# Attention ahead of two feed-forward layers: converting weights two steps later, and sums, loads, maxima and keys in a new order

## The chip, the cores and the metric

The kernel runs on one NeuronCore of a Trainium2 chip. The metric is the device time of one execution in microseconds (us), taken from the runs as they are; a further execution was recorded by the hardware profiler. Engines are named as the profile names them: PE (TensorE, matrix products), PEld (its weight loads), DVE (VectorE), ACT (ScalarE), POOL (GpSimd), SP (the queue that issues all DMAs). Each engine works through its own instructions strictly in the order in which the program lists them, and waits for others through semaphores.

## What is computed

The reference, cut to what matters (batch 2, 8 heads, 768 positions, head size 64; all float32):

```python
k_sum = k.reshape(B, H, nb, 32, D).max(axis=3)          # nb = 24 blocks
v_sum = v.reshape(B, H, nb, 32, D).mean(axis=3)
scores_l = scale * q @ k.T, kept where |i - j| < 16
scores_s = scale * q @ k_sum.T + log(32)
a = softmax(concat(scores_l, scores_s))
x = a @ concat(v, v_sum)                                 # 1536 tokens x 512
x = (g(x @ w_in)) @ w_out,  g(h) = h * cos(h)            # 512 -> 2048 -> 512
out = layernorm(h * softmax(h)) * g_ln @ w_out2, h = x @ w_in2   # 512 -> 1024 -> 512
```

The weights arrive as 64-bit floats, seen as pairs of 32-bit words, and are turned into float32 on the chip.

## The kernel before

**Stages.** Attention runs first, then the two feed-forward layers (FFN). The change lies in attention alone, and in the few FFN products that attention takes in between its own.

**Tiles of attention.** Two heads of one batch are a pair; there are 8 pairs (n = 0 to 7). A pair's 768 positions are three groups of four tiles of 64 queries, so there are 24 groups G = 3n + g. Each query tile sees a window of 96 keys and the 24 block summaries, 120 columns.

**The loop over steps.** Lines 663 to 741 are one loop with 29 steps (0 to 28), a software pipeline written out by hand: in step s the group s + 1 gets its scores while older groups are at later stages. In the order of the program a step holds:

- PE: the scores of group s + 1 (`emit_s`, L561, 16 products); the transposes of the probabilities of group s - 4 (`emit_t`, L598); where s = 3n + 2, the transposes of keys and queries of pair n + 2 (`emit_k` L494, `emit_q` L533); `fill` (L355: some first products of the FFN, L277, as the table `FILL` says); the product with v of group s - 5 (`emit_av`, L613); the block sums of v of a pair, in the steps that `VSUM_AT` lists (`sum_v`, L472, 24 products).
- DVE: the maxima of group s (`emit_max`, L572), the block maxima of keys (`emit_ksum`, L506) where the step has them, the sums of group s - 2 (`emit_sum`, L585, L586), the **join** of a weight's two words (`join_one`, L169), and, in every step with s = 3n + 1, the copies that lay the heads of keys and of queries of pair n + 2 side by side (`pair_k`, `pair_q`, both L426, tiles `kg` and `qg`). PE transposes these copies in the following step.
- ACT: the ends of the key windows (`emit_kx_ends`, L522, L525; first in the step for the pairs in `KX_FIRST`), the exponential of group s - 1 (L581), the high part of a joined weight (L186), the eviction of the transposed probabilities (`emit_at`, L603), the two **rebias** operations on a weight's words (`rebias_one`, L162, L163), the eviction of the result into `X` (L627), then key windows (`emit_kx`, L515), query rows (L547), high parts of `X` (L246) and the scaled block sums (`scale_v`, L480) where the step has them.
- POOL: the low part of a split weight (L187), the subtraction of the maxima of group s (L576), the normalisation of group s - 2 (L591), and the low part of a slice of `X` in steps 7, 10, 13 and 16 (`XS`, L247).
- SP: the loads of weights, keys, queries and v, and the copies that **place** the block sums into the tile of v (`place_vsum`, L487, at the start of the step after `scale_v`).

**A weight's way.** Attention converts the first 8 weight tiles. In a step listed in `WSTEPS` a tile is opened (`weights.bits`: its load, and that of the next one, is issued if it was not before). In the step after it ACT rebiases and DVE joins it; in the step after that ACT and POOL split it into a high and a low part. `load(0)` is issued apart, in step 2.

**PSUM banks.** Scores, transposed probabilities and results use four banks. The tile `qk` (three banks, one buffer) holds a pair's transposed keys and queries until ACT and DVE have read them. The bank `h` holds the block sums of v of pairs 0 to 5 and, from step 15 on, the first FFN product; the block sums of pairs 6 and 7 use `qk`. From step `QK_DONE` on, the three banks of `qk` are given to FFN products.

Two lines fix the order on DVE that the steps follow: `weights.finish()` (the join, L711) stands ahead of `pair_k(n + 2)` and `pair_q(n + 2)` (L732, L733) in the loop's body.

Of the kernel before, what the change touches and what calls it, by code (L numbers as in the profile page):

```python
# [7 lines left out]
F32 = mybir.dt.float32  # L8
# [16 lines left out]
def strided(t, offset, dims):  # L25

    return bass.AP(t.tensor, t.offset + offset, [list(t.ap[0])] + [list(d) for d in dims])
# [7 lines left out]
def fused_kernel(  # L35
# [15 lines left out]
    P = 128  # L51
    B, H, S, D = q.shape
# [39 lines left out]

    wide = w_in.dtype == mybir.dt.int64
    LOWEST = -3.0e38
    WSTEPS = (4, 7, 10, 13, 15, 16, 18, 19)
    XS = (7, 10, 13, 16)
    IDLE = (0, 0, 0)
    DVE_X = 19
    DVE_NORM = 99
    LAST = 5  # L100
    QK_DONE = 20
    REBIAS = float(2.0 ** -112)
    NEGATIVE = float(2.0 ** 32)
    TOP3 = float(0.936 * 2.0 ** -29)
# [165 lines left out]
    def h_products(step):  # L270
        fg, tb, f = work[step]
        h = h_of[step] = h_tile(step)
        m = 0
        for c in range(KC):
            for (a, b_) in PASSES:
                w = weights.done[w1[fg][0][c]]
                nc.tensor.matmul(  # L277
                    h, lhsT=w[:, a, f * P:(f + 1) * P], rhs=xs_of[tb, c][:, b_, :],
                    start=(m == 0), stop=(m == 3 * KC - 1))
                m += 1  # L280
                yield
# [54 lines left out]
    ps_h0 = ps_stack.enter_context(tc.tile_pool(name="ps_h0", bufs=1, space=PSUM))  # L336
    qk_stack = ps_stack.enter_context(ExitStack())
    ps_qk = qk_stack.enter_context(tc.tile_pool(name="ps_qk", bufs=1, space=PSUM))
# [3 lines left out]
    def warm_up(n):  # L342

        if not n:
            return
        idle = idles[0]
        t = ps_h0.tile([P, 512], F32, tag="h", name="idle")
        for _ in range(n):
            nc.tensor.matmul(t, lhsT=idle[:, 0:P], rhs=idle, start=True, stop=True)


    FILL = {15: 3, 16: 3, 17: 3, 18: 3, 20: 4, 21: 4, 22: 4, 23: 4, 24: 4, 25: 4, 26: 4, 27: 4, 28: 4}
    early = (x for step in range(GF) for x in h_products(step))

    def fill(step):  # L355

        if step == QK_DONE:
            qk_stack.close()
            ps_h[0] = ps_stack.enter_context(tc.tile_pool(name="ps_h", bufs=3, space=PSUM))
        for _ in range(FILL.get(step, 0)):  # L360
            next(early, None)
# [23 lines left out]
    def attention():  # L385
        st = ExitStack()
        with st:
# [41 lines left out]
            def pair_k(n):  # L429
                k_t[n] = side_by_side(k_t[n], "kg", nc.gpsimd if n == 1 else nc.vector)  # L430
# [30 lines left out]
            def blocks_of(t):  # L461
                at = FIRST if t == 0 else FINAL if t == NT - 1 else MID + 2 * HALF - 2 * (t % HALF)
                return strip[0:WIN, at:at + D]

            def sum_v(n):

                o = (ps_h0 if n < 6 else ps_qk).tile(
                    [P, 512] if n < 6 else [P, 2, 2, S // 2], F32, tag="h" if n < 6 else "qk", name="vsum")
                o = (o if n < 6 else o[:, 0, 0])[:, 0:P]
                for t in range(HALF):  # L470
                    for c in range(2):
                        nc.tensor.matmul(  # L472
                            o[D * c:D * c + D], lhsT=blocks_of(HALF * c + t),
                            rhs=v_t[n][0:WIN, HALF * c + t].rearrange("p j d -> p (j d)"),
                            start=(t == 0), stop=(t == HALF - 1))
                vs_t[n] = o
# [27 lines left out]
            def emit_ksum(n):  # L504
                ksum = io.tile([P, NS], F32, tag="ksum", name="ksum")
                nc.vector.tensor_reduce(  # L506
                    out=ksum, in_=strided(qk_t["k", n], 0, [[BLOCK // 2, NS], [S // 2, 2], [1, BLOCK // 2]]),
                    op=ALU.max, axis=AX.XY)
                ks_t[n] = ksum
# [56 lines left out]
            def emit_max(G):  # L566
                g = G % GPP
                sm = sm_t[G] = sms[G % NSM]
                sps = ss_t.pop(G)
                mx = sm_p.tile([P, NG], F32, tag="mx", name="mx")  # L570
                for i in range(NG):
                    nc.vector.tensor_tensor_reduce(  # L572
                        out=sm[:, i, 0:KW], in0=sps[:, i, :], in1=mask[:, (NG * g + i > 0) + (NG * g + i == NT - 1), :], scale=1.0, scalar=LOWEST,
                        op0=ALU.add, op1=ALU.max, accum_out=mx[:, i:i + 1])
                sm = sm[:, :, 0:KW]
                nc.gpsimd.tensor_tensor(  # L576
                    out=sm, in0=sm, in1=mx.unsqueeze(2).to_broadcast([P, NG, KW]), op=ALU.subtract)
# [5 lines left out]
            def emit_sum(G):  # L583
                ss = sm_p.tile([P, NG], F32, tag="ss", name="ss")
                nc.vector.tensor_reduce(out=ss, in_=sm_t[G], op=ALU.add, axis=AX.X)  # L585
                nc.vector.reciprocal(out=ss, in_=ss)  # L586
                sum_t[G] = ss
# [41 lines left out]
            NPAIR = B * NP  # L629
            NGR = NPAIR * GPP  # L630
# [26 lines left out]


            LX, LN, LT, LA = 1, 2, 4, 5
            KX_FIRST = (1, 2, 3, 4, 5)  # L660
            VSUM_AT = {1: 0, 5: 1, 8: 2, 10: 3, 13: 4, 14: 5, 16: 6, 19: 7}
            VLOAD_AT = {1: 1, 4: 2, 6: 3, 8: 4, 10: 5, 13: 6, 16: 7}
            for step in range(NGR + LA):
                n, g = divmod(step, GPP)
                summed = LN <= step < NGR + LN
                ahead = 1 if step == 1 else n + 1 if g == 0 and 0 < n < NPAIR - 1 else 0

                warm_up(IDLE[g] if step < min(FILL) else 0)
                if step - 1 in VSUM_AT:
                    place_vsum(VSUM_AT[step - 1])  # L670
                if step + 1 < NGR:
                    emit_s(step + 1)
                if step == 0:
                    pair_k(1)
                    emit_max(0)
                    pair_q(1)
                    emit_k(1)
                    emit_q(1)
                if LT <= step < NGR + LT:
                    emit_t(step - LT)  # L680
                if g == 2 and n + 2 < NPAIR:
                    emit_k(n + 2)
                    emit_q(n + 2)
                fill(step)
                if step >= LA:
                    emit_av(step - LA)
                if step in VSUM_AT:
                    sum_v(VSUM_AT[step])

                if g == 1 and n in KX_FIRST:  # L690
                    emit_kx_ends(n + 1)
                if step == NGR:
                    emit_at(step - LT)
                if LX <= step < NGR + LX:
                    emit_exp(step - LX)
                weights.split()
                if 0 < step < NGR:
                    emit_max(step)
                if LT <= step < NGR + LT and step != NGR:
                    emit_at(step - LT)  # L700
                if g == 1 and 0 < n < NPAIR - 1 and n not in KX_FIRST:
                    emit_kx_ends(n + 1)
                if ahead:
                    emit_ksum(ahead)
                if summed:
                    emit_sum(step - LN)
                if step == NGR + 3:
                    emit_x(step - LA)
                weights.rebias()
                drain(step - NGR, 0)  # L710
                weights.finish()  # L711
                if summed:
                    emit_norm(step - LN)
                if step >= LA and step != NGR + 3:
                    emit_x(step - LA)
                drain(step - NGR, 1)
                if ahead:
                    emit_kx(ahead)
                if step == 1:
                    emit_kx_ends(1)  # L720
                    emit_qx(1)
                if g == 2 and n + 2 < NPAIR:
                    emit_qx(n + 2)
                if step == 2:
                    weights.load(0)
                if step in WSTEPS:
                    weights.bits()
                for c in range(KC):
                    if step == XS[c]:
                        xs_of[0, c] = split_x(0, c, xs_a)  # L730
                if g == 1 and n + 2 < NPAIR:
                    pair_k(n + 2)  # L732
                    pair_q(n + 2)  # L733

                if g == 1 and n + 3 < NPAIR:
                    load_k(n + 3)
                    load_q(n + 3)
                if step in VLOAD_AT:
                    load_v(VLOAD_AT[step])
                if step in VSUM_AT:  # L740
                    scale_v(VSUM_AT[step])

# [682 lines left out]
```

## Time and profile before

| what | us |
|---|---|
| median of 3 runs (477.47, 478.20, 482.47) | 478.2 |
| the profiled execution | 477.52 |
| its span, first to last instruction | 475.7 |
| attention in it: PE's last attention product ends, FFN's line 319 begins | 97.11 |
| busy in the span: PE / DVE / ACT / POOL | 467.1 / 317.6 / 314.4 / 227.3 |

Busy time is the time in which an engine has an instruction under way. In a timeline a row gives the start in us from the span's start, the duration in us, engine, line, operation and tiles (written <- read); a number in brackets is the idle time of the engine just before it, with what ended it. Neighbouring instructions overlap a little at their ends, so the distance of two starts is the better measure of what one costs.

### The profile page before, as it was taken

What the parts mean: (1) busy time and instruction counts of PE and PEld (TensorE: products, weight loads), DVE (VectorE), ACT (ScalarE), POOL (GpSimd) and SP (SyncE); (2) the same over time, 40 slices, a digit from 0 to 9 for tenths busy, and PEclk for the clock granted to TensorE, in tenths of its full rate; (3) what the DMA queues carried; (4) which work ended last, traced back from release to release, by engine and by line L of the source; (5) the groups of instructions that cost most, each with busy time, mean ns of one, the idle gap of its engine ahead of it and who ended that gap; (6) DMA issues with size and microseconds to landing.
All of it is one profiled execution on the core that took longest, in us unless ns stands there. A gap on an engine that the chain in (4) does not pass through costs nothing.

```text
span 475.7 us, 8064 instructions
## 1 busy us (share of the span) xinstructions
PE 467.1 (98%) x2899; PEld 384.2 (81%) x2899; DVE 317.6 (67%) x754; ACT 314.4 (66%) x558; POOL 227.3 (48%) x230
## 2 busy tenths in 40 slices
PE   8999999999999999999999999999999999999997
PEld 4788877788888888888888888888888888888886
DVE  3989965663554456566464647474799999988930
ACT  3689888757675866556665456664872448888891
POOL 2689988424322222222223723655105878795450
PEclk9999999999999999999999999999999999999999
DMA  7999875001223222233222122110210031436351
GB/s 210 269 230 248 219 182 177 12 1 45 90 95 116 99 88 90 90 113 108 90 88 88 45 88 87 49 45 1 88 45 1 22 84 28 119 59 113 88 133 68
DMA packets 61304, 46.52 MB, mean 98 GB/s; under 512 B 42704, under 2 KB 53712, under 8 KB 61264
## 3 DMA queue, kind: packets, MB, share of 16 engines
q1 hardware_dynamic: 61264, 46.01, 34.3%
q8 instruction: 23, 0.38, 0.3%
q14 instruction: 17, 0.14, 0.1%
HBM read 36.43 MB, written 3.15 MB: 83 GB/s over the span
## 4 chain that ended last, share of the span: by engine, by line
PE 88%; POOL 4%; DVE 3%; DMA 2%; ACT 1%; issue 1%; SPq 0%; DVEq 0%; POOLq 0%
PE y L319 27%; PE h L277 27%; PE h L1074 14%; PE h L907 12%; PE sps L561 2%; PE ops L613 2%; PE aps L598 1%; POOL sm L576 1%; PE vsum L472 1%; POOL sm L591 1%; DMA qt<-in_q_dram 1%; DMA raw<-in_moe_w_out_dram 1%; POOL w L187 1%; DVE sm L572 1%; DVE ksum L506 1%
## 5 line engine op out<-in xcount | busy, mean ns | idle before, releaser
L277 PE MATMUL h<-xs,w 128*128 128x512 f32 x576 | 141.2, 391 | 0.0
L319 PE MATMUL y<-gs,w 128*128 128x512 f32 x576 | 138.2, 389 | 0.0
L319 PEld LDWEIGHTS y<-gs,w 128*128 128x128 f32 x576 | 108.0, 188 | 22.4
L277 PEld LDWEIGHTS h<-xs,w 128*128 128x128 f32 x576 | 107.2, 188 | 21.6
L187 POOL TENSOR_TENSOR w<-s,w 128x512 fp32r<-128x512 f32 x32 | 41.7, 1303 | 97.1 <-ACT w L186 95.1
L286 ACT ACTIVATE r<-h 128x512 int32<-128x512 f32 x48 | 28.6, 597 | 87.1 <-PE h L277 87.1
L291 DVE SCALAR_TENSOR_TENSOR r<-r,h 128x512 f32<-128x512 int32 x48 | 32.9, 686 | 71.0 <-ACT r L286 70.8
L1074 PE MATMUL h<-w,ls 128*128 128x512 f32 (+1 forms) x312 | 66.8, 374 | 0.0
L169 DVE SCALAR_TENSOR_TENSOR s<-raw 128x512 int32<-128x512 int32 x48 | 37.7, 786 | 40.5 <-ACT raw L163 39.2
L1074 PEld LDWEIGHTS h<-w,ls 128*128 128x128 f32 x312 | 55.3, 188 | 10.9 <-POOL ls L1051 0.6
L907 PE MATMUL h<-w,xo 128*128 128x512 f32 x252 | 58.7, 390 | 0.0
L907 PEld LDWEIGHTS h<-w,xo 128*128 128x128 f32 x252 | 47.1, 188 | 9.7
L296 ACT ACTIVATE r<-r,half_pi 128x512 f32<-128x512 f32 x48 | 34.5, 720 | 5.4 <-DVE r L291 5.3
L307 DVE TENSOR_TENSOR gs<-h,gs 128x512 fp32r<-128x512 f32 x48 | 32.6, 680 | 5.3 <-ACT gs L306 5.3
L301 DVE TENSOR_TENSOR h<-h,r 128x512 f32<-128x512 f32 x48 | 33.0, 688 | 4.0 <-ACT r L296 3.9
L162 ACT ACTIVATE raw<-raw 128x512 f32<-128x512 f32 x48 | 32.0, 667 | 1.0 <-DMA raw<-in_moe_w_out_dram 1.0
L778 POOL TENSOR_TENSOR w<-s,w 128x512 fp32r<-128x512 f32 x14 | 17.9, 1294 | 30.9 <-ACT w L777 30.9
L163 ACT ACTIVATE raw<-raw 128x512 int32<-128x512 uint32 x48 | 32.0, 666 | 0.0
L576 POOL TENSOR_TENSOR sm<-sm,mx 128x480 f32<-128x480 f32 x24 | 24.7, 1031 | 8.7 <-DVE mx L572 8.7
L306 ACT ACTIVATE gs<-h 128x512 fp32r<-128x512 f32 x48 | 28.2, 587 | 0.4 <-DVE h L301 0.3
L1044 ACT ACTIVATE s<-turned 128x1024 uint16<-128x1024 uint16 x20 | 26.5, 1367 | 2.3 <-POOL xo L895 1.8
L591 POOL TENSOR_TENSOR sm<-sm,ss 128x480 f32<-128x480 f32 x24 | 27.2, 1134 | 1.4 <-DVE ss L586 1.3
(105 smaller groups left out, 667.8 us busy)
## 6 DMA issues: line engine op xcount, KB each, us to landing
raw<-in_moe_w_in_dram SPq DMA_DIRECT2D x24, 512.0 KB, 3.7
raw<-in_moe_w_out_dram SPq DMA_DIRECT2D x24, 512.0 KB, 3.4
vt<-in_v_dram SPq DMA_DIRECT2D x16, 240.0 KB, 5.3
kt<-in_k_dram SPq DMA_DIRECT2D x8, 384.0 KB, 3.2
qt<-in_q_dram SPq DMA_DIRECT2D x8, 384.0 KB, 7.8
out_dram<-osb SPq DMA_DIRECT2D x11, 256.0 KB, 2.1
vt<-vm SPq DMA_DIRECT2D x16, 72.0 KB
vt<-in_v_dram SPq DMA_DIRECT2D x16, 48.0 KB, 6.0
```

The source lines that it names most:

```text
L162: nc.scalar.activation(out=hw, in_=hw, func=AF.Prelu, scale=REBIAS, alpha=NEGATIVE)
L163: nc.scalar.activation(out=lw, in_=lw.bitcast(U32), func=AF.Copy, scale=TOP3)
L169: nc.vector.scalar_tensor_tensor(out=self.f32[i], in0=t[:, :, 1], scalar=3, in1=t[:, :, 0], op0=ALU.logical_shift_left, op1=ALU.bitwise_or)
L187: nc.gpsimd.tensor_tensor(out=w[:, 1, :], in0=f, in1=as32(w[:, 0, :]), op=ALU.subtract)
L277: nc.tensor.matmul(h, lhsT=w[:, a, f * P:(f + 1) * P], rhs=xs_of[tb, c][:, b_, :], start=(m == 0), stop=(m == 3 * KC - 1))
L291: nc.vector.scalar_tensor_tensor(out=r, in0=r.bitcast(I32), scalar=TWO_PI, in1=h_of[step], op0=ALU.mult, op1=ALU.subtract)
L296: nc.scalar.activation(out=r, in_=r, func=AF.Sin, scale=-1.0, bias=half_pi)
L301: nc.vector.tensor_tensor(out=h, in0=h, in1=r, op=ALU.mult)
L307: nc.vector.tensor_tensor(out=gs[:, 1, :], in0=r, in1=as32(gs[:, 0, :]), op=ALU.subtract)
L319: nc.tensor.matmul(y[e], lhsT=w[:, a, e * P:(e + 1) * P], rhs=gs[:, b_, :], start=(f == 0 and i == 0), stop=(f == GF - 1 and i == 2))
L907: nc.tensor.matmul(banks_of[p][BANK[m]], lhsT=x[:, a, s0:s0 + P], rhs=w2_of[m, c][:, b_, :], start=c == j == 0, stop=c == 1 and j == 2)
L1074: nc.tensor.matmul(o, lhsT=ls_of[t][f // 4][:, a, s0:s0 + P], rhs=w[:, b_, cols], start=(f == 0 and i == 0), stop=(f == NF2 - 1 and i == 2))
```

## The change

The diff is whole. What it does:

- `WSTEPS`: each of the eight weights is opened, rebiased, joined and split two steps later. Rebias and join, which stood in steps 5, 8, 11, 14, 16, 17, 19 and 20, stand in 7, 10, 13, 16, 18, 19, 21 and 22. `load(0)` moves from step 2 to step 4.
- `FILL`: the 48 FFN products that stood in steps 15 to 18 (3 each) and 20 to 28 (4 each) stand in steps 19 to 28 (6, 6, 5, 5, 5, 5, 4, 4, 4, 4). `QK_DONE` moves from 20 to 21.
- `sum_v`: pair 6's block sums use bank `h`, as pairs 0 to 5 do. `VSUM_AT`: pair 1's sums move from step 5 to 4, pair 4's from 13 to 12, pair 5's from 14 to 15, pair 6's from 16 to 18, pair 7's from 19 to 20.
- `VLOAD_AT`: the loads of v of pairs 2, 4 and 5 move one step later, and stand behind the placing of pairs 1, 2 and 3 on SP.
- Step 2: `emit_max(3)` (of step 3) comes right after `emit_max(2)`; the block maxima and the windows of the third pair's keys (`emit_ksum(2)`, `emit_kx(2)`), of step 3 before, come in step 2, ahead of that pair's query rows on ACT.
- `KX_FIRST` takes in 6: the key ends of pair 7 come first in step 19 on ACT.

```diff
--- before.py
+++ after.py
@@ -92,13 +92,13 @@
 
     wide = w_in.dtype == mybir.dt.int64
     LOWEST = -3.0e38
-    WSTEPS = (4, 7, 10, 13, 15, 16, 18, 19)
+    WSTEPS = (6, 9, 12, 15, 17, 18, 20, 21)
     XS = (7, 10, 13, 16)
     IDLE = (0, 0, 0)
     DVE_X = 19
     DVE_NORM = 99
     LAST = 5
-    QK_DONE = 20
+    QK_DONE = 21
     REBIAS = float(2.0 ** -112)
     NEGATIVE = float(2.0 ** 32)
     TOP3 = float(0.936 * 2.0 ** -29)
@@ -349,7 +349,7 @@
             nc.tensor.matmul(t, lhsT=idle[:, 0:P], rhs=idle, start=True, stop=True)
 
 
-    FILL = {15: 3, 16: 3, 17: 3, 18: 3, 20: 4, 21: 4, 22: 4, 23: 4, 24: 4, 25: 4, 26: 4, 27: 4, 28: 4}
+    FILL = {19: 6, 20: 6, 21: 5, 22: 5, 23: 5, 24: 5, 25: 4, 26: 4, 27: 4, 28: 4}
     early = (x for step in range(GF) for x in h_products(step))
 
     def fill(step):
@@ -464,9 +464,9 @@
 
             def sum_v(n):
 
-                o = (ps_h0 if n < 6 else ps_qk).tile(
-                    [P, 512] if n < 6 else [P, 2, 2, S // 2], F32, tag="h" if n < 6 else "qk", name="vsum")
-                o = (o if n < 6 else o[:, 0, 0])[:, 0:P]
+                o = (ps_h0 if n < 7 else ps_qk).tile(
+                    [P, 512] if n < 7 else [P, 2, 2, S // 2], F32, tag="h" if n < 7 else "qk", name="vsum")
+                o = (o if n < 7 else o[:, 0, 0])[:, 0:P]
                 for t in range(HALF):
                     for c in range(2):
                         nc.tensor.matmul(
@@ -657,13 +657,13 @@
 
 
             LX, LN, LT, LA = 1, 2, 4, 5
-            KX_FIRST = (1, 2, 3, 4, 5)
-            VSUM_AT = {1: 0, 5: 1, 8: 2, 10: 3, 13: 4, 14: 5, 16: 6, 19: 7}
-            VLOAD_AT = {1: 1, 4: 2, 6: 3, 8: 4, 10: 5, 13: 6, 16: 7}
+            KX_FIRST = (1, 2, 3, 4, 5, 6)
+            VSUM_AT = {1: 0, 4: 1, 8: 2, 10: 3, 12: 4, 15: 5, 18: 6, 20: 7}
+            VLOAD_AT = {1: 1, 5: 2, 6: 3, 9: 4, 11: 5, 13: 6, 16: 7}
             for step in range(NGR + LA):
                 n, g = divmod(step, GPP)
                 summed = LN <= step < NGR + LN
-                ahead = 1 if step == 1 else n + 1 if g == 0 and 0 < n < NPAIR - 1 else 0
+                ahead = step if step in (1, 2) else n + 1 if g == 0 and 1 < n < NPAIR - 1 else 0
 
                 warm_up(IDLE[g] if step < min(FILL) else 0)
                 if step - 1 in VSUM_AT:
@@ -694,16 +694,20 @@
                 if LX <= step < NGR + LX:
                     emit_exp(step - LX)
                 weights.split()
-                if 0 < step < NGR:
+                if 0 < step < NGR and step != 3:
                     emit_max(step)
+                if step == 2:
+                    emit_max(3)
                 if LT <= step < NGR + LT and step != NGR:
                     emit_at(step - LT)
                 if g == 1 and 0 < n < NPAIR - 1 and n not in KX_FIRST:
                     emit_kx_ends(n + 1)
-                if ahead:
+                if ahead and step != 2:
                     emit_ksum(ahead)
                 if summed:
                     emit_sum(step - LN)
+                if step == 2:
+                    emit_ksum(2)
                 if step == NGR + 3:
                     emit_x(step - LA)
                 weights.rebias()
@@ -721,7 +725,7 @@
                     emit_qx(1)
                 if g == 2 and n + 2 < NPAIR:
                     emit_qx(n + 2)
-                if step == 2:
+                if step == 4:
                     weights.load(0)
                 if step in WSTEPS:
                     weights.bits()
```

## Rows read from the trace of the kernel before

**Rows 1.** The page, part 1: busy us of each engine

```profile
PE 467.1 (98%) x2899; PEld 384.2 (81%) x2899; DVE 317.6 (67%) x754; ACT 314.4 (66%) x558; POOL 227.3 (48%) x230
```

**Rows 2.** Windows: span, busy PE, PEld, DVE, ACT, POOL, granted clock, DMA

```profile
5.88:97.11 91.23, 86.98 (x1203) 70.52 (x1201) 71.56 (x287) 72.35 (x145) 67.96 (x63) 1.00 0.72 191
...
130.00:200.00 70.00, 70.00 (x311) 57.96 (x310) 36.90 (x57) 46.33 (x86) 16.24 (x13) 1.00 0.30 98
```

**Rows 3.** Waits of PE, 5 to 100 us: total, times, longest

```profile
...
PE sps L561 <- ACT kx L525: 1.2, 1, 1.2
...
PE vsum L472 <- ACT kx L522: 0.8, 1, 0.8
PE aps L598 <- POOL sm L591: 0.3, 1, 0.3
...
```

**Rows 4.** Timeline of PE, steps 5 to 8: start, us, [idle <-releaser]

```profile
21.29 1.04 PE L561 MATMUL sps<-kx,qx 64*64 64x120 f32 x16 [1.17 <-ACT kx L525]
...
24.16 0.87 PE L533 MATMUL qk<-ident,qg 128*128 128x128 f32 x6 [0.39 <-DVE qg L426]
...
25.48 1.48 PE L472 MATMUL vsum<-vt,strip 96*64 96x128 f32 x24
26.89 1.04 PE L561 MATMUL sps<-kx,qx 64*64 64x120 f32 x16
...
29.06 1.04 PE L561 MATMUL sps<-kx,qx 64*64 64x120 f32 x16
...
31.22 1.04 PE L561 MATMUL sps<-kx,qx 64*64 64x120 f32 x16
...
33.34 0.82 PE L533 MATMUL qk<-ident,qg 128*128 128x128 f32 x6
```

**Rows 5.** Timeline of DVE, step 16: join, copies of keys and queries

```profile
62.69 0.69 DVE L169 SCALAR_TENSOR_TENSOR s<-raw 128x512 int32<-128x512 int32 x1 [3.71 <-ACT raw L163]
63.30 0.55 DVE L426 COPY kg<-kt 128x768 f32<-128x768 f32 x1
63.77 1.63 DVE L426 COPY qg<-qt 128x768 f32<-128x768 f32 x1
```

**Rows 6.** Timeline of ACT in step 16: rebias

```profile
61.39 0.71 ACT L162 ACTIVATE raw<-raw 128x512 f32<-128x512 f32 x1
61.96 0.70 ACT L163 ACTIVATE raw<-raw 128x512 int32<-128x512 uint32 x1
```

**Rows 7.** Timeline of PE, step 17: the last pair's queries

```profile
65.46 0.88 PE L533 MATMUL qk<-ident,qg 128*128 128x128 f32 x6 [0.44 <-DVE qg L426]
```

**Rows 8.** Timeline of ACT in step 7

```profile
31.41 0.61 ACT L603 ACTIVATE at<-aps 120x512 f32<-120x512 f32 x1
31.89 0.41 ACT L627 ACTIVATE X<-ops 128x256 f32<-128x256 f32 x1
```

**Rows 9.** DVE lines 169 and 426, 14 to 97 us: ns min/median/max

```profile
L169 DVE SCALAR_TENSOR_TENSOR s<-raw x8: 691/714/1384, 25.6 to 78.6; 128x512 int32<-128x512 int32 x8
...
L426 DVE COPY qg<-qt x6: 560/1339/1634, 15.1 to 63.8; 128x768 f32<-128x768 f32 x6
```

**Rows 10.** Timelines of DVE and POOL: copy of queries in step 1, POOL's next

```profile
15.06 0.56 DVE L426 COPY qg<-qt 128x768 f32<-128x768 f32 x1 [0.42 <-DMA qt<-in_q_dram]
...
16.51 0.99 POOL L576 TENSOR_TENSOR sm<-sm,mx 128x480 f32<-128x480 f32 x1 [2.95 <-DVE mx L572]
```

**Rows 11.** DMA packets in 0 to 20.5 us and in 0 to 21 us

```profile
DMA packets 9577, 4.69 MB, mean 229 GB/s; under 512 B 5051, under 2 KB 9575, under 8 KB 9575
...
DMA packets 9654, 4.74 MB, mean 226 GB/s; under 512 B 5052, under 2 KB 9649, under 8 KB 9652
```

**Rows 12.** Timeline of SP: placing pair 1's block sums

```profile
28.35 1.66 SPq L487 DMA_DIRECT2D vt<-vm  x2
```

**Rows 13.** The page, part 6: DMA issues, KB each, us to landing

```profile
vt<-in_v_dram SPq DMA_DIRECT2D x16, 240.0 KB, 5.3
```

**Rows 14.** The page, part 5: the subtraction of a split weight on POOL

```profile
L187 POOL TENSOR_TENSOR w<-s,w 128x512 fp32r<-128x512 f32 x32 | 41.7, 1303 | 97.1 <-ACT w L186 95.1
```

## The prediction

> **What bounds the kernel now.** I read the page's busy times first. PE is busy for 467.1 of 475.7 us [rows 1], so time can only come or go where PE has a gap, and the windows say where to look: from 130 us on a stretch of 70 us holds 70.00 us of PE, while attention, from 5.88 to 97.11 us, holds 86.98 of 91.23 [rows 2]. Everything behind attention is one unbroken row of products, so whatever moves the end of attention moves the end of the kernel by as much. Next the waits of PE inside attention [rows 3]: one of 1.2 us for the key windows, one of 0.8 for key ends, one of 0.3 for a normalised group. The timeline puts them in place: 1.17 us ahead of the scores of step 5, and 0.39 for copied queries in the same step; without extras a step takes 29.06 to 31.22 = 2.16 us of PE, and the block sums of v add 25.48 to 26.89 = 1.41 [rows 4]. So attention is PE's work plus small gaps, and the question is which gaps go and which come.
>
> The row that decides my forecast is step 16, the only step of before in which a join and the copies of the next keys and queries meet. DVE stood still for 3.71 us until ACT had rebiased, then joined (62.69), copied keys (63.30) and queries (63.77, 1.63 us) [rows 5]. ACT's two rebias operations had begun at 61.39 and ended at 61.96 + 0.70 = 62.66 [rows 6], 0.03 us ahead of the join. PE, one step on, waited 0.44 us for those queries [rows 7], although its own step 16 was long (three FFN products and the sums of a pair).
>
> **The change, part by part.**
>
> *Conversions two steps later.* This removes nothing: eight rebias pairs, joins and splits stay. But the joins that stood in steps 5, 8, 11 and 14 come to stand in 7, 10 and 13 (and the one of step 16 is again in 16), and 7, 10, 13 and 16 are the very steps with `pair_k` and `pair_q`, behind the join in DVE's order. Queued behind the waiting join are those two copies and the next maxima; for the copies waits PE, with all its later work behind. Step 7, from the step's start T on PE: ACT's order there is the same as before up to the eviction L603, after which its next instruction began at 31.89, that is T + 2.83 [rows 8, 4]. There the rebias now goes in: 61.96 - 61.39 + 0.70 = 1.27 us, ending at T + 4.10. Join from T + 4.13, 0.61 to the keys (T + 4.74), 0.47 to the queries (T + 5.21), then a copy of queries of 1.34, the median [rows 9]: T + 6.55, and PE takes it 0.05 later, at T + 6.60. PE would be ready for these transposes at 33.34 in before, T + 4.28 [rows 4]. Wait A: 2.3 us. Step 10 has the sums of pair 3 besides, so PE is ready at T + 4.28 + 1.41 = 5.69: wait B 0.9. Steps 13 and 16 are plain steps of 2.16 now (the sums of pairs 4, 5 and 6 have left 13, 14 and 16 for the steps ahead or later), and with sums at the end of the step before, ACT has its key windows behind it; what holds ACT is then PE's own transposes, some 1.6 into the step, one eviction (31.89 - 31.41 = 0.48, [rows 8]) and the rebias, so the join begins at about T + 3.4, the queries are ready at T + 5.87, PE is ready at T + 4.28: waits C and D 1.6 each. Sum 2.3 + 0.9 + 1.6 + 1.6 = 6.4 us.
>
> Bounds. Below: ACT never behind in any of the four steps (join at T + 3.4) and the copy at its shortest, 0.56: queries at T + 5.1, waits 0.8 + 0 + 0.8 + 0.8 = 2.4. Above: join at its longest, 1.38, and copy at 1.63 [rows 9]: 1.06 more in each step, 6.4 + 4.2 = 10.6. I take 6.4, since the join of step 16 ran at its short length and the median of the copies is a long one.
>
> The copy of queries took 0.56 in step 1, where POOL was idle for 2.95 us up to 16.51, and 1.34 or more in the others [rows 10]. The Trainium skill, Advanced Engine Details and Errata, section VectorE Performance Modes, notes that VectorE's second SBUF port is shared with GpSimd, so that the two block each other in VectorE's two-port modes. By that rule the copy is long just where POOL has work beside it, as `XS` gives it in these four steps; were POOL idle during them, the waits would come to 6.4 - 4 x 0.78 = 3.3.
>
> *Third keys and fourth maxima, sums of pair 1 in step 4.* I take it that the key windows come no sooner: ACT now holds them, and with them its wait for the keys' maxima, ahead of the query rows and the exponential, which it did in that wait before. But the sums of pair 1, 1.41, now stand on PE inside the gap of 1.17. They need v of pair 1. Its packets are of 256 bytes; the count of packets under 512 bytes stands at 5051 at 20.5 us and rises by 1 to 21 [rows 11], so it has arrived by about 20.7. PE is free at 21.29 - 1.17 = 20.12, would run the sums from 20.7 to 22.1, and start the scores of step 5 there. From those scores to step 6 it was 26.89 - 21.29 = 5.60 [rows 4], less the sums and the wait of 0.39 that falls away: 3.80, so step 6 starts at 25.9. Gain 1.0. With v there by 20.12 the queries' copy still ends near 24.1, and 24.16 + (26.89 - 24.16 - 1.41) = 25.5 is the best, gain 1.4; with v at 21.5 it is 0.2. The order of maxima costs nothing: both scores are there, and POOL's next normalisation still ends just ahead of its transposes.
>
> *Seventh sums in bank `h`, later sums, key ends first.* The sums of pairs 6 and 7 no longer wait behind key ends in `qk`: the 0.8 goes. The 0.44 of step 17 goes too, being counted anew in wait D. What is late next is the first FFN product of step 19, which needs ACT's eviction of pair 6's sums from `h`, at the end of a full ACT step; PE reaches it 1.5 into step 19: I take nothing, 1.0 at most.
>
> *First FFN products later.* 48 before and after, no cost by themselves. Five instead of four in steps 23 and 24 put PE's work ahead of the transposes that waited 0.3 for POOL [rows 3]: gain 0.3.
>
> *Loads of v behind placing.* On SP, v of pair 2 now stands behind the placing of pair 1, which waits for sums that end at 22.1 and takes 1.66 [rows 12]; it goes out from about 24.1, with the keys and queries of later pairs behind it. A load of v lands 5.3 us after its issue [rows 13], by 30; the sums that need it stand in step 8, behind the queries of 33.34 [rows 4]. The weight loads queued with it are needed two steps later than before. Cost nothing; were that cover gone, PE would wait for v as long as it lands behind 33.3.
>
> Sum on the profiled execution: 477.5 + 6.4 - 1.0 - 0.8 - 0.4 - 0.3 = 481.4 us. The profiled execution lies 0.7 below the median of the runs shown, inside their spread, so I forecast 481.4.
>
> **The rivals.**
>
> *Gaps go and none comes (not slower).* If the joins find their words ready or the copies stay ahead of PE, as with the joins of steps 8, 11 and 14 that never reached PE, all gains stand: 477.5 - 2.5 = 475.0. Against it: those joins had no copies behind them, and step 16 has. It decides from the point where the join starts before T + 1.8 in a plain step.
>
> *Long joins and copies.* All four waits at their upper bounds, 10.6, give 477.5 + 10.6 - 2.5 = 485.6. For it: POOL, freed of waits, works beside DVE more. Against: the blocked DVE starves POOL too.
>
> *Short copies.* POOL lives on what DVE hands it; if DVE's wait for the join leaves POOL idle as in step 1, the copies take 0.56 as there: 481.4 - 4 x 0.78 = 478.3. Against: POOL's split of `X` follows the same rebias on ACT and falls on the copy. The skill's rule on the shared port is what would make it so.
>
> *The tail.* Two more weights are split on POOL in steps 22 and 23, 1.3 us each [rows 14], ahead of the last subtractions; PE already waits 0.3 there. If the last of them lands on that path: 481.4 + 1.3 + 0.3 = 483.0.
>
> **How the numbers follow.** Forecast 0.58; no new gap 0.12; long copies 0.13; short copies 0.07; tail 0.10. The forecast's own range, with each wait half a microsecond off, is 479.4 to 483.4. The range 475.5 to 485.0 leaves out most of the first rival and more than half of the second, together some 0.2. A change of 1%, 4.8 us, is what a measurement of this kernel can tell from none: faster than that needs 473.4, below the best case, 0.03; slower, above 483.0, is the second rival, half of the tail and the upper edge of the forecast, 0.23; within 0.74.
>
> **What would show it.** Right: in the waits of PE, keys (L494) and queries (L533) for DVE L426 four times, together 5 to 7 us, in the steps 8, 11, 14 and 17; in DVE's timeline a join ahead of the copies each time, idle before it for ACT L163; no wait of PE for L522 and none of over 1 us for L525; attention's end near 101.0 instead of 97.11. Wrong: PE's keys and queries without waits, or a wait of PE for v (DMA), for ACT L480 in step 19, or for POOL L591 in the tail of over 0.5 us; a granted clock below full anywhere.

## The result, and the profile after

| what | before | after |
|---|---|---|
| median of 9 runs each (lowest, highest), us | 478.20 (477.19, 482.47) | 483.69 (482.14, 485.34) |
| profiled execution, us | 477.52 | 483.99 |
| attention's end, where line 319 begins, us | 97.11 | 103.12 |

The ratio of after to before is 1.010, with a 95% interval from 1.0067 to 1.0133. The change makes the kernel some 5 us slower, and the interval lies on both sides of the 1% mark. Of the 6.5 us between the profiled executions 6.0 had come about by the end of attention.

After: the page's busy time [rows 1], then the waits of PE inside attention, 5 to 110 us [rows 3] (us in total, times, longest):

```profile
PE 470.0 (97%) x2899; PEld 385.8 (80%) x2899; DVE 318.1 (66%) x754; ACT 314.2 (65%) x558; POOL 225.0 (47%) x230
```

```profile
PE qk L494 <- DVE kg L426: 3.5, 4, 1.5
PE qk L533 <- DVE qg L426: 2.7, 4, 0.7
PE vsum L472 <- DMA vt<-in_v_dram: 0.3, 1, 0.3
PE aps L598 <- POOL sm L591: 0.3, 1, 0.3
...
```

The waits for key windows (L525, 1.2) and key ends (L522, 0.8) are gone, the 0.3 for POOL stands, and the copies are waited for eight times, 6.2 us together. PE's busy time rose by 2.9 us although it has the same 2899 products: some of them ran longer, as the windows below show, or lost the overlap with the product ahead of them.

After: timeline of PE [rows 4]. Each L561 row is the start of a step (the first scores, then steps 6 to 8, 9, 11, 12 and 13 to 15), and L494 and L533 are the transposes of copied keys and queries:

```profile
9.31 1.86 PE L561 MATMUL sps<-kx,qx 64*64 64x120 f32 x32 [0.23 <-DVE qx L543]
...
25.21 1.04 PE L561 MATMUL sps<-kx,qx 64*64 64x120 f32 x16
27.38 1.04 PE L561 MATMUL sps<-kx,qx 64*64 64x120 f32 x16
29.54 1.04 PE L561 MATMUL sps<-kx,qx 64*64 64x120 f32 x16
...
32.68 0.87 PE L494 MATMUL qk<-ident,kg 128*128 128x128 f32 x6 [1.52 <-DVE kg L426]
34.23 1.54 PE L533 MATMUL qk<-ident,qg 128*128 128x128 f32 x6 [0.68 <-DVE qg L426]
...
38.42 1.04 PE L561 MATMUL sps<-kx,qx 64*64 64x120 f32 x16
...
44.06 1.04 PE L561 MATMUL sps<-kx,qx 64*64 64x120 f32 x16
...
48.87 1.04 PE L561 MATMUL sps<-kx,qx 64*64 64x120 f32 x16
...
52.35 1.04 PE L561 MATMUL sps<-kx,qx 64*64 64x120 f32 x16
54.52 1.04 PE L561 MATMUL sps<-kx,qx 64*64 64x120 f32 x16
57.02 0.87 PE L494 MATMUL qk<-ident,kg 128*128 128x128 f32 x6 [0.89 <-DVE kg L426]
58.58 0.88 PE L533 MATMUL qk<-ident,qg 128*128 128x128 f32 x6 [0.68 <-DVE qg L426]
60.00 1.04 PE L561 MATMUL sps<-kx,qx 64*64 64x120 f32 x16
```

Before, the same view gave the length of such steps without a wait: step 8, with block sums, 36.01 - 31.22 = 4.79 (its start is in [rows 4]), and step 11, without, 45.13 - 41.66 = 3.47:

```profile
36.01 1.04 PE L561 MATMUL sps<-kx,qx 64*64 64x120 f32 x16
...
41.66 1.04 PE L561 MATMUL sps<-kx,qx 64*64 64x120 f32 x16
...
45.13 1.04 PE L561 MATMUL sps<-kx,qx 64*64 64x120 f32 x16
```

So step 8 of after, 38.42 - 29.54 = 8.88, lost 4.1 us; step 11, 4.81, lost 1.3; step 14, 5.48, lost 2.0; and step 17 (5.49 from 65.64 to 71.13) 2.0 again. That is 9.4 us of lost time where the view of waits shows 6.2 of idle time. The difference has two parts. Step 8 has a slow stretch. These are the windows of after; the columns are stretch, length, busy PE, PEld, DVE, ACT, POOL, then the granted clock, DMA share and GB/s:

```profile
34.00:36.00 2.00, 1.77 (x12) 1.44 (x14) 1.97 (x14) 0.00 (x0) 2.00 (x2) 0.50 0.86 203
36.00:38.00 2.00, 2.00 (x36) 2.00 (x33) 0.62 (x7) 1.09 (x2) 2.00 (x3) 0.65 0.47 169
```

Behind the gaps of 1.52 and 0.68 us the granted clock fell to 0.50, the 1.2 GHz level, and the transposes of queries took 1.54 in place of 0.82. The other part is 0.2 us for each wait, which the experiment with the split of `X` shows below.

After: DVE in steps 7 and 16 [rows 5], and POOL beside the first:

```profile
31.47 0.69 DVE L169 SCALAR_TENSOR_TENSOR s<-raw 128x512 int32<-128x512 int32 x1 [1.66 <-ACT raw L163]
32.07 0.55 DVE L426 COPY kg<-kt 128x768 f32<-128x768 f32 x1
32.54 1.63 DVE L426 COPY qg<-qt 128x768 f32<-128x768 f32 x1
...
66.94 0.69 DVE L169 SCALAR_TENSOR_TENSOR s<-raw 128x512 int32<-128x512 int32 x1 [2.35 <-ACT raw L163]
67.55 0.55 DVE L426 COPY kg<-kt 128x768 f32<-128x768 f32 x1
68.02 1.64 DVE L426 COPY qg<-qt 128x768 f32<-128x768 f32 x1
```

```profile
32.30 1.46 POOL L247 TENSOR_TENSOR xs<-X,xs 128x512 fp32r<-128x512 f32 x1 [1.09 <-ACT xs L246]
```

Join, copy of keys and copy of queries stand in this order behind ACT's rebias, and DVE is idle until it comes. Steps 10 and 13 show the same three rows (44.68 and 55.80, idle 3.33 and 2.35).

### The profile page after: what moved, and what is told of

Read it like the earlier page. It is cut to its first block, busy times and chain, and to the rows that moved or that the text cites. A ratio compares the mean times of both kernels' runs of the same rounds, so it can differ in the third digit from the quotient of the medians.

```text
span 482.2 us, 8067 instructions
## 1 busy us (share of the span) xinstructions
PE 470.0 (97%) x2899; PEld 385.8 (80%) x2899; DVE 318.1 (66%) x754; ACT 314.2 (65%) x558; POOL 225.0 (47%) x230
## 4 chain that ended last, share of the span: by engine, by line
PE 84%; DVE 5%; ACT 4%; DMA 3%; issue 2%; POOL 1%; SPq 1%; POOLq 0%; ACTq 0%; DVEq 0%
PE y L319 27%; PE h L277 26%; PE h L911 12%; PE h L1078 10%; PE sps L561 2%; PE ops L613 2%; PE vsum L472 1%; PE aps L598 1%; DVE qg L426 1%; DMA vt<-in_v_dram 1%; PE qk L533 1%; DMA qt<-in_q_dram 1%; ACT at L603 1%; ACT kx L515 1%; DMA vt<-vm 1%
## 5 line engine op out<-in xcount | busy, mean ns | idle before, releaser
L247 POOL TENSOR_TENSOR xs<-X,xs 128x512 fp32r<-128x512 f32 x10 | 14.0, 1405 | 28.8 <-ACT xs L246 28.8
L591 POOL TENSOR_TENSOR sm<-sm,ss 128x480 f32<-128x480 f32 x24 | 24.7, 1029 | 5.7 <-DVE ss L586 5.2
```

## The experiments

My theory: the joins that stand ahead of the copies on DVE make PE's eight waits. The rivals: another part of the change costs the time, the length of the copies decides, or the clock does. Medians are of the runs of one kernel; each ratio is to the kernel before on the same chip, with its 95% interval.

**Conversions alone, and conversions back.** To the kernel before, only `WSTEPS`, the place of `load(0)`, `FILL` and `QK_DONE` of the change:

> The kernel before with the conversions two steps later, and the first FFN products in their later steps because they need the converted weights; nothing else. By the joins: steps 8 and 11 lose as in the changed kernel (about 4 and 1.3 us), steps 14 and 17 less, since sums of v still stand in steps 13 and 16 and give the copies 1.4 us more; 481.5 to 484. If the other parts lose the time: 477 to 479.

Measured: 483.56 us, 1.0117 (1.0092 to 1.0142). Its waits of PE, 5 to 104 us:

```profile
PE qk L533 <- DVE qg L426: 3.0, 5, 0.7
PE qk L494 <- DVE kg L426: 2.3, 4, 1.5
PE sps L561 <- ACT kx L525: 1.2, 1, 1.2
```

This part alone makes the kernel as slow as the whole change does, with the waits for copies there and the old wait for key windows still in place. The reverse, the changed kernel with the old conversion steps:

```diff
-    WSTEPS = (6, 9, 12, 15, 17, 18, 20, 21)
+    WSTEPS = (4, 7, 10, 13, 15, 16, 18, 19)
...
-                if step == 4:
+                if step == 2:
                     weights.load(0)
```

> The changed kernel with the conversions in their old steps (and the first weight load in step 2); every other part of the change stays. If the joins ahead of the copies made the loss, three of the four waits of PE for copied keys and queries go (steps 8, 11, 14) and the one of step 17 stays, since a join stands in step 16 either way: before's 477.5, less 1.4 for the start, 0.8 for the seventh sums, plus about 1.5 for the larger wait in step 17, so 476 to 477.5. If the other parts (sums, loads, maxima, keys) lose the time, it stays above 481.

Measured: 481.15 us, 1.0056 (1.0035 to 1.0077), a miss by some 4 us. Steps 8, 11 and 14 have no wait for copies any more, but one join and two copies still meet in step 16, as they do before [rows 5]. Its PE, the starts of steps 16 and 17 and then step 17, and DVE, step 16:

```profile
56.66 1.04 PE L561 MATMUL sps<-kx,qx 64*64 64x120 f32 x16
...
58.83 1.04 PE L561 MATMUL sps<-kx,qx 64*64 64x120 f32 x16
...
63.14 0.88 PE L494 MATMUL qk<-ident,kg 128*128 128x128 f32 x6 [2.69 <-DVE kg L426]
64.69 1.15 PE L533 MATMUL qk<-ident,qg 128*128 128x128 f32 x6 [0.68 <-DVE qg L426]
...
66.83 1.86 PE L561 MATMUL sps<-kx,qx 64*64 64x120 f32 x16
```

```profile
60.43 1.11 DVE L169 SCALAR_TENSOR_TENSOR s<-raw 128x512 int32<-128x512 int32 x1 [2.50 <-ACT raw L163]
61.46 1.62 DVE L426 COPY kg<-kt 128x768 f32<-128x768 f32 x1
63.01 1.63 DVE L426 COPY qg<-qt 128x768 f32<-128x768 f32 x1
```

Step 17 takes 8.00 us for 3.47: this one meeting costs 4.5 us, 3.4 of it idle, and from 66 to 68 us the granted clock is 0.50. In the kernel before PE waited 0.44 there [rows 7]. Two things differ. PE's step 16 of before holds three FFN products and block sums, which the rest of the change takes away; I had left that cover out of the expectation. And the chain on DVE is longer: the join takes 1.11 for 0.69 and the copy of keys 1.62 for 0.55, so that the queries' transposes start 8.03 after PE's step 16 does (64.69 - 56.66) for 6.89 before (65.46 - 58.57). Neither was tried by itself. The clock also has a part in the miss: nine of the ten executions have a mean granted clock of 0.992 to 0.996, and the one at 1.000 took 478.44 us.

**The order on DVE.** The changed kernel, with the two copies moved ahead of the join in the loop's body (step 1 left as it is):

```diff
                 weights.rebias()
                 drain(step - NGR, 0)
+                if g == 1 and 0 < n and n + 2 < NPAIR:
+                    pair_k(n + 2)
+                    pair_q(n + 2)
                 weights.finish()
```

> The changed kernel with one order turned on VectorE: in steps 4, 7, 10, 13 and 16 the copies of keys and queries stand ahead of the join. The conversions stay as late as the change put them. If the order is the cause, the four waits for copies go and with them the slow restart: 474 to 476. If late conversions burden ScalarE and GpSimd and the order does not matter, the waits stay and it is above 481.

Measured: 475.95 us, 0.995 (0.9924 to 0.9976), 7.7 below the changed kernel. All conversions are as late as in the change; only the order on DVE differs, no wait for copied keys is left, and for copied queries one of 0.2. Its largest wait of PE inside attention, and DVE in step 7:

```profile
PE h L277 <- ACT vm L480: 1.0, 1, 1.0
```

```profile
29.25 0.95 DVE L426 COPY kg<-kt 128x768 f32<-128x768 f32 x1
30.12 1.34 DVE L426 COPY qg<-qt 128x768 f32<-128x768 f32 x1
31.38 0.68 DVE L169 SCALAR_TENSOR_TENSOR s<-raw 128x512 int32<-128x512 int32 x1
```

The copies now fill the time in which DVE had waited for ACT, and the join is hardly later: 31.38 is 4.47 behind the start of PE's step 7 (26.91), for 4.09 in the change. The other way to the same end leaves the order alone and puts the conversions where no copies are:

```diff
-    WSTEPS = (6, 9, 12, 15, 17, 18, 20, 21)
+    WSTEPS = (4, 7, 10, 13, 16, 17, 19, 20)
```

(with `load(0)` in step 2)

> The changed kernel with the conversions opened in steps 4, 7, 10, 13, 16, 17, 19 and 20, so that no join stands in a step that copies keys and queries (joins in 5, 8, 11, 14, 17, 18, 20, 21). If the meeting of join and copies is all of the loss, no wait for copies is left and it runs like the kernel with the copies ahead of the join: 475 to 476, with the wait of about 1 us for pair 6's sums in step 19 still there. If the lateness of the conversions matters besides, the four early ones show it: it would differ from that kernel by over 1 us.

Measured: 476.11 us, 0.9933 (0.9908 to 0.9958). Its trace still has waits for copies in one step, the 8th, 0.4 for keys and 0.4 for queries. The meeting of join and copies is the cause, not the lateness of the conversions.

**The length of the copies.** The changed kernel with `XS = (8, 11, 14, 17)` for `(7, 10, 13, 16)`:

> The changed kernel with the slices of X split one step later (8, 11, 14, 17), so that GpSimd's 1.4 us subtraction no longer falls on VectorE's copy of queries. If the copy is long because GpSimd works beside it, it goes from 1.63 us to about 0.6 and each of the four waits for queries gets shorter by 0.7: 3 to 4 us below the changed kernel, near 480. If the copy's length has another cause, it stays 1.6 and the time 483.7.

Measured: 479.30 us, 1.0017 (0.999 to 1.0044). Its DVE in step 7, POOL's next instruction behind one that ended at 30.91, and PE in step 8:

```profile
31.17 0.69 DVE L169 SCALAR_TENSOR_TENSOR s<-raw 128x512 int32<-128x512 int32 x1 [1.66 <-ACT raw L163]
31.78 0.55 DVE L426 COPY kg<-kt 128x768 f32<-128x768 f32 x1
32.25 0.55 DVE L426 COPY qg<-qt 128x768 f32<-128x768 f32 x1
```

```profile
32.60 1.34 POOL L187 TENSOR_TENSOR w<-s,w 128x512 fp32r<-128x512 f32 x1 [1.69 <-ACT w L186]
```

```profile
29.25 1.04 PE L561 MATMUL sps<-kx,qx 64*64 64x120 f32 x16
32.39 0.88 PE L494 MATMUL qk<-ident,kg 128*128 128x128 f32 x6 [1.52 <-DVE kg L426]
...
35.77 1.04 PE L561 MATMUL sps<-kx,qx 64*64 64x120 f32 x16
```

The join is as late as in the change and PE waits 1.52 for keys as before, but with POOL idle the copy of queries takes 0.55 instead of 1.63 and nobody waits for it. The time is 4.4 below the changed kernel and 3.4 above the copies first, so the long copy behind the late join makes more of the loss than the late join by itself. The granted clock stays at 1.00 in this trace. With one wait in a step its whole price can be read: step 8 takes 6.52, that is 1.73 lost for 1.52 idle; steps 11 and 14 lose 0.44 and 1.12 for idle times of 0.21 and 0.90. So a wait cost 0.2 us more than its idle time here: neighbouring products overlap by 0.16 us (transposes of 0.82 follow each other after 0.66), and behind a gap they don't.

**The clock.** The changed kernel with six idle products (`warm_up(6)`) ahead of the transposes of keys in step 8, twice, the second time beside the unaltered changed kernel:

> The changed kernel with six idle products of 0.22 us on TensorE in step 8, ahead of the keys, in the gap of 1.5 us that it waits there anyway. In the changed kernel's trace the granted clock fell in that step and the queries, products and sums behind the gap took 4.2 us where other steps need 2.7. If the gap lets the clock fall, it stays full here and the run is 1 to 1.5 us below the changed kernel's, near 482.3. If the fall has nothing to do with the gap, the time is that of the changed kernel, 483.7.

> The changed kernel once more, beside the next three on one chip. All theories: about 483 us, a profile with a granted clock near 0.50 in a part of step 8. It is there as the base of the next run: the theory that the clock's fall costs about 1 us net wants it that much above the kernel with idle products in that gap.

> The changed kernel with six idle products ahead of the transposes of keys in step 8. If the clock's fall costs time: 1.0 to 1.5 us below the changed kernel of the same call, that is near 482, with the clock at 1.00 through step 8 and the waits for kg and qg left as they were elsewhere. If the fall is only a mark of the gap and costs nothing: equal to it within 0.5 us.

Measured: idle products 482.78 us, ratio 1.0101 (1.0078 to 1.0124), and the second time 483.10, 1.0091 (1.0067 to 1.0115); changed kernel again 483.49, 1.0092 (1.0066 to 1.0118). The pair is not told apart, and the reason is in the trace of the repeated kernel, PE and windows:

```profile
30.31 1.04 PE L561 MATMUL sps<-kx,qx 64*64 64x120 f32 x16
33.44 0.88 PE L494 MATMUL qk<-ident,kg 128*128 128x128 f32 x6 [1.51 <-DVE kg L426]
34.99 0.88 PE L533 MATMUL qk<-ident,qg 128*128 128x128 f32 x6 [0.67 <-DVE qg L426]
37.73 1.04 PE L561 MATMUL sps<-kx,qx 64*64 64x120 f32 x16
```

```profile
34.00:36.00 2.00, 1.33 (x15) 0.92 (x15) 2.00 (x10) 0.48 (x1) 2.00 (x2) 1.00 0.34 72
```

The same gaps, and the clock did not fall: step 8 takes 7.42 for 8.88. So the fall comes in some executions, and cost 1.46 us in this step. The 15 executions of the changed kernel divide by their mean granted clock: six at 0.999 or 1.000, median 482.5 us, and nine at 0.992 to 0.996, median 484.0. With idle products 11 of 12 stay at 0.999 or 1.000: the fall becomes rarer. The median of all twelve is 483.0, for 483.6 of the fifteen; why the eleven, at 482.9, are not nearer to 482.5 isn't shown, since step 8 takes 7.45 us in the first trace with the products, no more than without a fall. Which stretch the other executions lost their clock in isn't shown; only the mean is. The kernel before has such executions too: of the 64 taken beside these experiments nine are at 0.995 or 0.996, with a median of 481.3 us for 478.4 of the others. A fall is more frequent in the changed kernel, then, but the gaps of step 8 are not its only occasion.

**The start alone.** To the kernel before, only the fourth maxima and third keys in step 2, pair 1's sums in step 4 and the load of v of pair 2 in step 5:

> The kernel before with the start of the change alone: fourth maxima and third keys in step 2, pair 1's sums of v in step 4, v of pair 2 loaded in step 5. By the forecast the gap of 1.17 us in step 5 and that of 0.39 for the queries go, and the sums wait some 0.3 for v: 1.0 to 1.4 us below before, 476.5 on a before of 477.5 to 478. The rival, that the later key windows, or v of pair 2 behind the placing, cost as much as that gains: no difference.

Measured: 477.54 us, 0.9968 (0.9946 to 0.999), 0.9 below: smaller than expected, and a gain.

**What was left over.** The wait for L480, 1.0 us with the copies first and 0.6 with the conversions clear of them, is for ACT's eviction of pair 6's sums from bank `h`. With these sums in step 17 instead of 18, first beside the conversions clear of the copies, then with the copies first:

> The kernel without joins at pair steps, with pair 6's sums of v in step 17 instead of 18, so that ScalarE's eviction of them from the bank of the first FFN product comes a step earlier. If that eviction makes the wait of 1.0 us in step 19, it goes: 474 to 475, faster than before by 0.7%. If the wait belongs to something else of that step, it stays and the time is that of the kernel beside it.

> Changed kernel, copies ahead of the joins on DVE, and the sums of pair 6 one step earlier. If the 1.0 us that PE waited for ACT L480 (pair 6's sums in bank h) in the run with copies first belongs to the place of those sums: that wait gone, about 475.0, 1 us below copies first alone (475.95). If ACT is late there for another reason: 476 and the wait moved to another product.

> The fastest version so far (conversions in steps clear of the copies, sums of pair 6 in step 17; 474.98) with the split of x also one step later. What is left of waits for copied queries there is 1.4 us in two places. If they are due to long copies beside GpSimd: copies near 0.55, no wait for qg in step 11, about 474.3. If these copies now meet other GpSimd work: 475, unchanged.

Measured: 474.98 us, 0.9919 (0.989 to 0.9948); 475.28, 0.9921 (0.9899 to 0.9944); and 475.67, 0.9932 (0.9908 to 0.9957). The wait for L480 is in none of the three traces. In the last one the copies of queries take 1.34 or 1.35 in all steps but the first, beside POOL's normalisations or its subtractions of maxima; without the later split they do so too, but for 1.63 in step 10. So the expected gain of the later split did not come. All three beat both kernels, by 3 to 4 us against before, and are not told apart.

## Why the prediction was right, and where it was off

The forecast of 481.4 was 2.3 below the median, which lies 0.3 above the forecast's own range and inside the whole one.

*The joins and copies.* The mechanism was right in every row. The join of step 7 was put at T + 4.13 and began at 31.47 - 27.38 = T + 4.09; that of step 16 at about T + 3.4, and began at T + 3.46; from join to queries it is 1.07, as forecast from 0.61 and 0.47. The mis-sized term is the copy: "a copy of queries of 1.34, the median [rows 9]". It took 1.63 or 1.64, the long one of [rows 5], in all four steps. So the queries' transposes start at T + 6.85 (34.23 - 27.38) for T + 6.60, and in step 14 at T + 6.23 (58.58 - 52.35) for T + 5.87. Against the time at which PE would be ready, T + 4.28 or T + 5.69, the delays come to 2.57, 1.18, 1.95 and 1.95 for the 2.3, 0.9, 1.6 and 1.6 of the four waits, 7.6 for 6.4; with what follows in the steps 8.0 are lost at full clock. That the view of waits gives 6.2 and seems to meet the 6.4 is chance: it leaves out 0.2 for each of eight waits. The row of [rows 5] was the nearest one, as the only copy behind a late join; the median came from steps whose copy lies beside a normalisation or a subtraction of maxima. The upper bound of these waits has a slip: it sets the join's longest duration, 1.38, against a distance of starts, 0.61. Durations alone, 1.38 for 0.69, give 0.98 more in each step, 10.3 in all and 485.3 for 485.6.

*Short copies.* This rival was priced at 478.3. The experiment that gives its condition, POOL idle during the copies, gave 479.30, so POOL does make the copy long, and the rival's condition was absent: in the changed kernel the split of `X` does fall on the copy, as the argument against it said. The rule as the prediction put it, long "just where POOL has work beside it", is too wide: the copy of keys in step 7 has L247 beside it from 32.30 on and takes 0.55. What counts is which of the two begins first (last section).

*The start.* Step 6 starts 25.21 - 9.31 = 15.9 after the first scores, for 26.89 - 9.57 = 17.3 before: 1.4 gained for 1.0, the "best" of the working, since the v of pair 1 held PE only 0.3. Alone and by medians it was 0.9. The 1.4 is the luck of one execution: in the trace of the repeated changed kernel PE waits 0.9 for that v and takes 16.5 to step 6 (25.98 - 9.51), and the twelve traces with the new start lie between 15.8 and 17.1.

*Sums of pairs 6 and 7, and the old wait of step 17.* Both waits went. "I take nothing, 1.0 at most" for the first FFN product of step 19 held in the changed kernel, where PE was late by itself; with the delay gone the bound came true, at 1.0.

*The 0.3 of POOL* did not go: `PE aps L598 <- POOL sm L591` stands. Behind attention there is one new wait of 0.3 (a product of line 1078, for POOL's line 1055), and the rest of the kernel is 0.46 longer than before; what brings that about wasn't tried. The tail rival's price, 1.6, was not paid.

*The clock* was named as a sign of error, "a granted clock below full anywhere", and stood in no term. The nine of fifteen executions that show it have a median 1.5 us above the other six.

The sum with measured terms: 477.5 + 8.0 (waits) - 1.4 (start) - 0.8 - 0.4 = 482.9, or up to 0.4 less, if the two waits removed also cost 0.2 more than they showed. The executions at full clock have a median of 482.5. With the 1.46 of step 8 the sum comes to 484.0 to 484.4, for 483.99 in the profiled execution. Attention's end, forecast near 101.0, came at 103.12 for the same reasons.

## What to carry to other kernels

Before a step is moved on an in-order engine, look at what stands behind it there in its new step: a wait for another engine costs nothing in a step where nothing urgent follows, and ahead of a copy that the busiest engine needs it costs whatever that engine can't fill with work of its own (here 1.3 to 2.6 us a step at full clock). The remedy costs no work: put the urgent instructions ahead of the one that waits. For the size of a shared resource's cost take the row with the same neighbour, not the median; and price a new gap on PE as its idle time, plus the lost overlap, plus what a fall of the clock takes.

## What the runs showed of the hardware that I had not expected

A copy's length is set by the POOL instruction that is under way when it begins. In step 7 of after POOL's L247 ends at 32.30 + 1.46 = 33.76, and the copy of queries at 32.54 + 1.63 = 34.17. This is POOL in step 16 of before:

```profile
63.52 1.47 POOL L247 TENSOR_TENSOR xs<-X,xs 128x512 fp32r<-128x512 f32 x1 [1.28 <-ACT xs L246]
```

It ends at 64.99, and the copy of [rows 5] at 65.40. Both copies end 0.41 after POOL does, and one that begins with POOL idle takes 0.55 in all. It is so in all fourteen traces: from 12 to 80 us each L426 copy on DVE that begins with a POOL instruction under way ends 0.40 to 0.46 after that instruction (one, begun as the next POOL instruction took over, 0.42 after the next), and each that does not takes 0.53 to 0.57. The Trainium skill, SBUF — State Buffer, section "SBUF: two separate sides", says of the port pair that VectorE, in a two-port mode, and GpSimd share that whichever comes first holds it for its whole instruction and that the other blocks. These rows agree, from the other side too: the copy of keys, begun at 32.07, keeps its 0.55, and L247, begun at 32.30 beside it, takes 1.46, for 1.27 where no copy is near (at 36.26 in the run with the later split of `X`).

The granted clock can fall to 0.50 behind two gaps of 1.5 and 0.7 us, and need not: the same program with the same gaps kept 1.00 in another execution. One gap of 1.52 alone, in the trace with the later split of `X`, and pairs of 0.89 and 0.68 us, in steps 14 and 17 of after, left it at full; so did gaps of 1.53 and 0.67 us in the run of the conversions alone.
